# Output product of an RWKV-7 + SoLU kernel: products 320 columns wide in one run, and another order of a slot's transposes

## The chip, the cores and the metric

One core of one Trainium2 chip. The metric is the device time of one execution in microseconds (us). Three runs of the kernel before are on record: 533.9, 535.26 and 539.12 us, median 535.26 us. One further execution was taken with the hardware profiler; its span from the first to the last instruction is 536.5 us, which is 1.2 us above the median and within the spread of the runs.

## The reference

All arrays are float32 at first; the two weight matrices of the second part arrive as 64-bit floats and are converted in the kernel. The first part is a recurrence over 768 time steps for 4 batches and 8 heads of width 40; its output is laid out as 3072 rows of 320 columns and goes through a second part with 1024 hidden columns.

```
for t in range(S):                                   # S = 768
    y[:, :, t] = einsum('bhd,bhde->bhe', r_t, state)
    Sa = einsum('bhde,bhe->bhd', state, a_t)
    state = state * w_t - einsum('bhd,bhe->bhde', Sa, b_t) + einsum('bhd,bhe->bhde', v_t, k_t)
x = y.transpose(0, 2, 1, 3).reshape(3072, 320)
h = x @ w_in                                         # 320 x 1024
solu = h * softmax(h)
ln = (solu - mean(solu)) / sqrt(var(solu) + 1e-6) * g_ln
out = ln @ w_out                                     # 1024 x 320
```

## The kernel before

**Tiling.** The recurrence is cut into chunks of 64 steps. Two batches are worked at once, one on partitions 0 to 63 and one on 64 to 127, so there are N = 24 chunks (12 in time, 2 pairs of batches), each with 8 heads. Each chunk gives 128 rows of the second part. The order of all work on every engine is the order in which the program is written; nothing is rescheduled.

**Slots.** The main loop (L973) runs over slots i = -1 to 26. In one slot several chunks are in different stages: chunk i+5 has its a and b turned (`front`, `front_b`), chunk i+6 its decay (`decay_turned`), chunk i+7 its running sum of log decays (`decay_by_halves`); chunk i+1 has its k, v, r and the state turned (`attend_kv`, `attend_r`, `stated`), its scores and its solution prepared; chunk i is solved and read (`solved`, `read`, `summed`); chunk i-2 goes through `x @ w_in` (`hidden`) and the softmax and variance (`highest`, `exped`, `weighed`, `spreadof`); chunk i-3 has its normalised rows turned (`folded`, tile `lnT`) and multiplied by the output weights (`output`, tile `po`). The inverse that each chunk needs is worked out in small steps on VectorE (L508, L516, L519) which `vector(plan)` puts between the rest.

**Names.** PE (TensorE) turns a tile by `nc.tensor.transpose` into PSUM, and ScalarE (ACT) or VectorE (DVE) copies it to SBUF. The `turned` helper (L395 to L403) issues eight transposes for one operand. In the trace the destination names are: `pa` for a and b, `pkv` for k and v, `plnT` for the normalised rows, `pst` for the state and for the running sum (`pst<-lw`), `pb` for r and for the decay (`pb<-cst,ei`). The copies out of PSUM are `aT` and `bT` on DVE and `kvT`, `rT`, `ex`, `lnT`, `s`, and then `ei` and `inv` (both from the running sum) on ACT. `osb` is the scaled output product on its way from `po` to the output DMA. Then come `pu` (`solved`), `ps` (`scores`), `h` (`hidden`), `psr`, `py`, `px` and `pyo`.

**PSUM.** It is used as four pairs of banks by tag: A, B, C and h. From slot 5 on, B and C change places every slot under the names X and Y. In a slot, `pkv`, `pu` and `py` and the output product `po` at its end use Y; `pb`, `ps` and `px` use X; `pa`, `pst`, `psr` and `pyo` use A; `plnT` and `h` use the tag h, and so does the scrap output of the square `sq` (L790). A tile of a tag can be written when all readers of the tile before it in that tag have ended. `po`, written into Y at the end of one slot, is in the pair that is X in the next slot: `pb` of that slot comes after `osb` has read it.

**The output product.** `output` (L845) adds eight products over f, each of 128 rows of the hidden width by 320 output columns. `in_parts` (L289) splits each into two of 160 columns. A float32 product stands in the trace as two matmul records and two weight loads, so the eight products are 32 records (`po<-w,lnT ... 128x160`, 768 in all). With `FIRST = 6`, slots 5 to 22 issue six of the eight (24 records) at their end, and the other two (8 records) in the next slot, after the transposes of a, b, k and v; the closure `stored` then issues `osb` and the output DMA.

**The end of the loop.** Slot 25 issues seven of the eight products and slot 26 the rest; slot 26 also has the output product of the last chunk in its own function.

The lines of the loop that set the order, from slot 5 on, are L1012 to L1040.

Of the kernel before, what the change touches and what calls it, by code (L numbers as in the profile page):

```python
# [21 lines left out]
AHEAD = 5  # L22
LANDS_NEXT = {2: 6, 3: 7, 4: 8, 5: 11, 6: 9, 7: 10, 8: 12}
LAG = 2
EARLY = 10
NK = 5
FIRST = 6
SPLITS = {2: (0, 0, 0, 2, 4), 24: (0, 0, 0, 0, 2)}


# [23 lines left out]
def kernel(  # L54
# [24 lines left out]
    N = NPAIR * NCH  # L79
    NF = DFF // P  # L80
# [60 lines left out]
    w2 = const.tile([P, NF, DM], FP32, name="w2")  # L141
# [3 lines left out]
    def pair(tag, name):  # L145
        return psum.tile([P, 2, 512], FP32, tag=tag, name=name)
# [142 lines left out]
    def in_parts(o, lhsT, rhs, start, stop, n=2):  # L289
        width = rhs.shape[-1] // n  # L290
        for x in range(n):
            part = slice(width * x, width * x + width)
            mm(o[:, part], lhsT, rhs[:, part], start and not x, stop)
# [119 lines left out]
    def decay_turned(i, t=None, y=0):  # L413

        if not ok(i):
            return lambda: None
        ex = st[i]["ex"] = ex_t[i % (AHEAD + 2)]
        t = turned(pair("B", "pei") if t is None else t, y, ei_t[0])
        return lambda: nc.scalar.copy(out=ex[0:W2, :, :, 1:], in_=t)
# [165 lines left out]
    def attend_r(i, t, y):  # L585
        if not ok(i):
            return lambda: None
        t = turned(t, y, r_t[0])

        def evict():  # L590
            st[i]["rT"] = kept("rT", t)
        return evict
# [252 lines left out]
    def output(i, t, first=NF):  # L845
        if not ok(i):
            return
        d = st[i]
        bp, ci = where_(i)
        t = t[:, 0:DM]  # L850

        def products(lo, hi):
            for f in range(lo, hi):
                in_parts(t, d["lnT"][:, f, :], w2[:, f, :], f == 0, f == NF - 1)
        products(0, first)

        def stored():
            osb = two.tile([P, DM], FP32, tag="osb", name="osb", bufs=1)
            nc.scalar.mul(out=osb, in_=t, mul=d["rs"])
            for p in range(2):  # L860
                nc.sync.dma_start(out=out.rearrange("(b s) n -> b s n", b=B)[2 * bp + p, ci * C:ci * C + C], in_=osb[half(p)])
        if first < NF:
            rest.append((lambda: products(first, NF), stored))
        else:
            stored()
# [107 lines left out]
    for i in range(-1, N + LAG + 1):  # L973
        j, c = i + AHEAD, i - LAG
        plan = plans.get(i, plans[N + i % GRP])
        if len(plan) > 6:
            plan, unflipped = plan[:2] + plan[3:], plan[2]
        else:
            unflipped = ""
        steady = i >= EARLY - AHEAD  # L980
        if i >= 0 and not steady:
            load_keys(j + 3, "w")
        if not steady:
            load_r(i + 3)
        elif i > EARLY - AHEAD and i % GRP:
            load_r(i + 2)
        if i == -1:
            load_values(2)
            land(4, nc.sync)
            land(len(lands), nc.sync)  # L990

        if i < EARLY - AHEAD:
            tc_, ta = pair("C", "pa"), pair("A", "pb")
            front_out, r_out = front(j, ta, 0), attend_r(i + 1, ta, 1)
            fold_out = folded(c - 1)
            ei_out, b_out = decay_turned(j + 1, tc_, 0), front_b(j, tc_, 1)
            kv_out = attend_kv(i + 1, pair(turn["X"], "pkv"))
            r_out()
            front_out()
            if i < EARLY - AHEAD:  # L1000
                vector(plan[0])
                fold_out()
                b_out()
            else:
                b_out()
                vector(plan[0])
                fold_out()
            s_out = stated(i + 1, pair("A", "pst"), 0) if ok(i + 1) else lambda: None
            for evict in (ei_out, kv_out, s_out):
                evict()  # L1010
        else:
            turn.update(zip("XY", ("BC", "CB")[(i - EARLY + AHEAD) % 2]))  # L1012
            ta = pair("A", "pa")
            front_out, b_out = front(j, ta, 0), front_b(j, ta, 1)
            kv_out = attend_kv(i + 1, pair(turn["Y"], "pkv"))
            front_out()
            kv_out()
            b_out()
            if i == N + LAG:
                fold_out = folded(c - 1)  # L1020
            for products, stored in rest:
                products()
                if i == N + LAG:
                    late.append(stored)
                else:
                    stored()
            rest.clear()
            vector(plan[0])
            if i < N + LAG:
                fold_out = folded(c - 1)  # L1030
            ts = pair("A", "pst")
            s_out = stated(i + 1, ts, 0) if ok(i + 1) else lambda: None
            tc_ = pair(turn["X"], "pb")
            r_out, ei_out = attend_r(i + 1, tc_, 0), decay_turned(j + 1, tc_, 1)
            if i == EARLY - AHEAD and ok(j + 2):
                logged(j + 2)
            cum_out = decay_by_halves(j + 2, ts)
            for evict in (r_out, ei_out, fold_out, s_out, *late):
                evict()
            late.clear()  # L1040
        if not steady:
            left(i - 1)
        if i == EARLY - AHEAD:
            load_keys(j + 3, "w")

        early = i < EARLY - AHEAD or i > N - 2
        waves = (1, 0, 1, 0, 1, 0, 1, 1, 0, 0, 0) if early else (0, 0, 2, 1, 0, 0, 1, 1, 0, 0, 0)
        wave = iter(range(NK))

        def run(x):  # L1050
            for _ in range(waves[x]):
                hidden(c, next(wave))
            if sum(waves[:x + 1]) == NK and sum(waves[:x]) < NK:
                highest(c)

        run(0)
        if i >= EARLY - AHEAD:
            cum_out()
        solved(i)()
        vector(plan[1])  # L1060
        if not steady:
            load_keys(j + 2, "bak")
        run(1)
        scores(i + 1)()
        vector(unflipped)
        flip(i + 1)
        run(2)
        scaled(j + 1, "b")
        stated_r(i + 1)
        run(3)  # L1070
        norm(j)
        if ok(j) and j % GRP == GRP - 1:
            begin_inverse(j // GRP)
        scaled(j + 1, "k")
        by_value(i + 2)
        run(4)
        if i == LAG + 1:
            mean = mean_more(pair("A", "pmean")[:, 0], 6, NF, mean)
        carried(i + 1)
        run(5)  # L1080
        read(i, 0)
        if i >= 0:
            load_values(i + 3)
        if steady:
            left(i - 1)
            load_keys(j + 2, "ba" if i % GRP else "b")
            if i % GRP:
                load_r(i + 3)
        ahead = 2 + (i >= EARLY - AHEAD)
        if ok(j + ahead):  # L1090
            logged(j + ahead)
        vector(plan[2])
        run(6)
        couple(i + 1)()
        if i == LAG + 1:
            centred(mean)
        run(7)
        close(i + 1)
        run(8)
        driven(i + 1)()  # L1100
        run(9)
        read(i, 1)
        run(10)
        exped(c)
        vector(plan[3])
        finish = summed(i)
        vector(plan[4])

        if i < EARLY - AHEAD:
            decay(j + 2, pair("C", "pcum")[:, 0])()  # L1110
        tb = pair(turn["X" if i < EARLY - AHEAD else "Y"], "po")
        weighed(c)
        if i == N - 1:
            finish()
        spreadof(c)
        if i >= 0:
            some(Q, (i + 2) // GRP)
            odd = steady and i % GRP == 1
            if odd:
                load_keys(j + 2, "k")  # L1120
                load_keys(j + 4, "w")
            bring(i + 2)
            if odd:
                load_keys(j + 3, "ak")
                load_keys(j + 5, "w")
        if i != N - 1:
            finish()
        vector(plan[5])
        if i == N + LAG:
            output_last(c - 1)  # L1130
        else:
            output(c - 1, tb[:, 0], NF - 1 if i == N + LAG - 1 else FIRST if EARLY - AHEAD <= i < N - 1 else NF)
        if i == -1:
            turn_g(tb[:, 0])
        if i == LAG - 1:
            mean = mean_more(tb[:, 0], 0, 3)
        if i == LAG:
            mean = mean_more(tb[:, 0], 3, 6, mean)
# [30 lines left out]
```

## Time and profile before

| | |
|---|---|
| runs | 533.9, 535.26, 539.12 us; median 535.26 us |
| span of the profiled execution | 536.5 us |
| slots 6 to 17, each from the start of one `po` run to the next | 18.45 to 19.60 us |
| slots 18 to 22, likewise | 17.74, 17.13, 16.95, 16.96 and 16.96 us |
| granted TensorE clock, mean | 0.984 of full speed; 1.00 in every slot from 5 on |
| DVE busy in slots 6 to 17 | 14.97 to 18.86 us of each |
| ACT busy in slots 6 to 17 | 10.93 to 12.00 us of each |

How to read the profile: times are in us from the first instruction. A timeline row has its start, its length, the engine, the line, the operation, output<-inputs with shapes, the count of merged instructions, and in brackets the idle time of the engine just before and what ended it. PE records overlap, since matmuls are pipelined: the start of the next row, not the end of this one, tells how long a row keeps PE. A "busy" PE is therefore not always issuing; a wait shorter than the tail of the last matmul shows no idle time.

### The profile page before, as it was taken

The page shows a single profiled execution, that of the slowest core. Times are in us where ns is not written, and L with a number is a line of the kernel's source. Part 1 is how long each engine was busy: PE and PEld are TensorE (multiplying, and loading weights), DVE is VectorE, ACT ScalarE, POOL GpSimd, SP SyncE. Part 2 cuts the span into 40 slices and gives each one's busy share as a digit, 9 for nine tenths or more (in the row PEclk, how much of TensorE's full clock was granted, in tenths as well). Part 3 has the DMA queues.
Part 4 walks back from the last instruction along what each step waited for, and adds up shares of the span by engine and source line. Part 5 has one row for each costly group of instructions (what it writes and reads, how often), then busy time and mean ns, then how long its engine had stood idle before and what let it go on. Part 6 is the DMA issues. An engine that isn't in the chain of part 4 may idle for free.

```text
span 536.5 us, 28053 instructions
## 1 busy us (share of the span) xinstructions
PE 480.7 (90%) x12029; PEld 391.0 (73%) x12029; DVE 430.6 (80%) x1752; ACT 314.1 (59%) x627; POOL 227.0 (42%) x376
## 2 busy tenths in 40 slices
PE   4633775798989999999999999999999999999997
PEld 3522665665878878877887887788778877887766
DVE  4599987999997987997998979979989888544322
ACT  3633466488457566556666665666656555654433
POOL 4577538245253344545445263544445331210300
PEclk9999978799999999999999999999999999999999
DMA  8898889765465566674774776675554551421210
GB/s 149 153 157 160 177 142 206 165 134 124 90 131 120 102 125 138 123 151 96 147 156 104 132 150 121 118 155 109 114 118 102 108 111 43 106 65 29 61 53 24
DMA packets 194475, 63.95 MB, mean 119 GB/s; under 512 B 166840, under 2 KB 186528, under 8 KB 194352
## 3 DMA queue, kind: packets, MB, share of 16 engines
q1 hardware_dynamic: 181232, 41.60, 41.8%
q0 software_dynamic: 10768, 19.95, 15.2%
q8 instruction: 94, 1.54, 1.2%
q10 hardware_dynamic: 2352, 0.62, 0.7%
q14 instruction: 29, 0.24, 0.2%
HBM read 47.96 MB, written 14.16 MB: 116 GB/s over the span
## 4 chain that ended last, share of the span: by engine, by line
PE 73%; DVE 17%; DMA 5%; issue 2%; ACT 2%; SPq 0%; POOL 0%; ACTq 0%; POOLq 0%; DVEq 0%
PE po L285 20%; PE h L285 18%; PE px L285 6%; PE pyo L285 5%; PE py L285 5%; DVE prod L516 4%; PE ps L285 4%; DVE uu L519 3%; PE pu L285 3%; PE plnT L804 2%; PE pb L400 2%; PE pa L400 2%; PE psr L285 2%; PE pkv L400 2%; DMA uu_dram<-uu 1%
## 5 line engine op out<-in xcount | busy, mean ns | idle before, releaser
L285 PE MATMUL h<-w_in,xT 64*64 64x512 f32 (+1 forms) x1064 | 121.7, 551 | 0.7 <-issue 0.7
L285 PE MATMUL po<-w,lnT 128*128 128x160 f32 x768 | 115.2, 304 | 0.0
L516 DVE TENSOR_TENSOR prod<-blk,uu 128x48 f32<-128x48 f32 (+19 forms) x576 | 108.1, 227 | 1.3
L285 PEld LDWEIGHTS po<-w,lnT 128*128 128x128 f32 x768 | 105.5, 190 | 4.7 <-issue 0.8
L519 DVE TENSOR_TENSOR uu<-uu,prod 128x48 f32<-128x48 f32 (+19 forms) x576 | 103.8, 219 | 0.0
L483 POOL DMA_DIRECT2D nt_dram<-nt x86 | 50.8, 597 | 84.5 <-ACT nt L475 76.4
L792 POOL TENSOR_TENSOR rs<-var,mhalf 128x1 f32<-128x1 f32 x24 | 17.6, 734 | 138.2 <-ACT var L791 138.1
L761 DVE TENSOR_REDUCE nmax<-h 128x1 f32<-128x1024 f32 x24 | 29.3, 1219 | 32.9 <-PE h L285 32.9
L285 PEld LDWEIGHTS h<-w_in,xT 64*64 64x64 f32 x1064 | 36.7, 133 | 20.4 <-issue 16.7
L790 ACT ACTIVATE sq<-e,mu 128x1024 f32<-128x1024 f32 x24 | 26.9, 1119 | 24.4 <-DVE e L777 24.4
L444 DVE TENSOR_TENSOR lu<-pu,cst 128x512 f32<-128x512 f32 x24 | 16.5, 686 | 26.6 <-PE pu L285 24.8
L769 ACT ACTIVATE e<-h,nmax 128x1024 f32<-128x1024 f32 x24 | 26.7, 1111 | 17.7 <-DVE nmax L761 17.7
L558 ACT ACTIVATE wy<-py,cst 128x256 f32<-128x256 f32 x24 | 11.4, 474 | 39.2 <-PE py L285 37.1
L311 POOL DMA_DIRECT2D raw_r<-in_r_dram x48 | 33.3, 698 | 0.0
L777 DVE SCALAR_TENSOR_TENSOR e<-h,e 128x1024 f32<-128x1024 f32 x24 | 29.2, 1217 | 4.3 <-ACT e L769 4.1
L508 DVE SCALAR_TENSOR_TENSOR uu<-blk,uu 128x30 f32<-128x30 f32 (+3 forms) x144 | 30.2, 262 | 1.7 <-DMA blk<-nt_dram 0.8
L393 POOL TENSOR_TENSOR kb<-raw_b,inv 128x320 f32<-128x320 f32 x24 | 21.4, 894 | 21.1 <-DMA raw_b<-in_b_dram 13.7
L285 PE MATMUL pcum<-lw,cst 128*128 128x160 f32 x48 | 15.1, 461 | 16.7 <-ACT lw L351 16.7
L285 PEld LDWEIGHTS py<-tu,nt 64*64 64x64 f32 x768 | 17.3, 142 | 16.3 <-issue 10.7
L617 ACT COPY st<-psr 128x416 f32<-128x416 f32 (+1 forms) x44 | 14.2, 374 | 24.5 <-PE psr L285 24.4
L664 ACT ACTIVATE x<-px 128x832 f32<-128x832 f32 x24 | 20.7, 864 | 11.0 <-PE px L285 11.0
L710 DVE TENSOR_TENSOR tot<-pyo,st 104x416 f32<-104x416 f32 x44 | 23.8, 581 | 2.9 <-PE pyo L285 2.9
(154 smaller groups left out, 1095.3 us busy)
## 6 DMA issues: line engine op xcount, KB each, us to landing
xT<-x_dram SPq DMA_DIRECT2D x48, 160.0 KB, 4.2
blk<-nt_dram POOLq DMA_DIRECT2D x22, 256.0 KB, 4.7
raw_w<-in_w_dram SPq DMA_DIRECT2D x48, 80.0 KB, 3.3
raw_r<-in_r_dram POOLq DMA_DIRECT2D x48, 80.0 KB, 4.0
lv<-in_v_dram SPq DMA_DIRECT2D x48, 80.0 KB, 3.7
out_dram<-osb SPq DMA_DIRECT2D x46, 80.0 KB, 2.5
a<-in_a_dram SPq DMA_DIRECT2D x44, 80.0 KB, 4.0
raw_k<-in_k_dram SPq DMA_DIRECT2D x42, 80.0 KB, 3.8
```

What stands on the lines that cost most here:

```text
L285: nc.tensor.matmul(o, lhsT=lhsT, rhs=rhs, start=start, stop=stop, skip_group_check=True)
L311: queue.dma_start(out=x[half(p), :, 0:D], in_=ap[2 * bp + p, :, ci * C:(ci + 1) * C, :].rearrange("h t d -> t h d"))
L400: nc.tensor.transpose(out=t[0:W2, p, at + C * j:at + C * j + C], in_=x[half(p), 2 * j:2 * j + 2].rearrange("p a b -> p (a b)")[:, skip:ski ...
L483: queue.dma_start(out=blocks[n][e].rearrange("(a x h) s c -> a x s h c", a=GRP, x=2)[at, x], in_=nt[home:home + Q].rearrange("p h j c -> p ...
L508: nc.vector.scalar_tensor_tensor(out=u[:, c, j + 1:Q], in0=nb[:, j, j + 1:Q], scalar=u[:, c, j:j + 1], in1=u[:, c, j + 1:Q], op0=ALU.mult, ...
L516: nc.vector.tensor_tensor(out=ts[-1], in0=nb[:, j:j + 1, j + 1:Q].to_broadcast([P, hi - lo, m]), in1=u[:, lo:hi, j:j + 1].to_broadcast([P, ...
L519: nc.vector.tensor_tensor(out=u[:, lo:hi, j + 1:Q], in0=u[:, lo:hi, j + 1:Q], in1=x, op=ALU.add)
L710: nc.vector.tensor_tensor(out=by_b(tot)[:, :, :, part], in0=y[:, :, :, part], in1=by_b(state_of(i)[:, x])[:, :, :, 0:HW], op=ALU.add)
L761: nc.vector.tensor_reduce(out=nmax, in_=d["h"], axis=AX.X, op=ALU.max, negate=True)
L769: nc.scalar.activation(out=e, in_=d["h"], func=AF.Exp, bias=d["nmax"], accum_out=d["esum"])
L777: nc.vector.scalar_tensor_tensor(out=d["e"], in0=d["h"], scalar=1.0 / DFF, in1=d["e"], op0=ALU.mult, op1=ALU.mult, accum_out=d["mu"])
L790: nc.scalar.activation(out=pair("A" if i == N - 2 else "h", "sq").rearrange("p a b -> p (a b)"), in_=d["e"], func=AF.Square, scale=-float( ...
```

## The change

The diff against the kernel before:

```diff
-FIRST = 6
...
         def products(lo, hi):
             for f in range(lo, hi):
-                in_parts(t, d["lnT"][:, f, :], w2[:, f, :], f == 0, f == NF - 1)
+                mm(t, d["lnT"][:, f, :], w2[:, f, :], f == 0, f == NF - 1)
...
             kv_out()
             b_out()
-            if i == N + LAG:
-                fold_out = folded(c - 1)
+            fold_out = folded(c - 1)
             for products, stored in rest:
                 products()
-                if i == N + LAG:
-                    late.append(stored)
-                else:
-                    stored()
+                late.append(stored)
             rest.clear()
             vector(plan[0])
-            if i < N + LAG:
-                fold_out = folded(c - 1)
+            tc_ = pair(turn["X"], "pb")
+            r_out, ei_out = attend_r(i + 1, tc_, 0), decay_turned(j + 1, tc_, 1)
             ts = pair("A", "pst")
             s_out = stated(i + 1, ts, 0) if ok(i + 1) else lambda: None
-            tc_ = pair(turn["X"], "pb")
-            r_out, ei_out = attend_r(i + 1, tc_, 0), decay_turned(j + 1, tc_, 1)
...
-            for evict in (r_out, ei_out, fold_out, s_out, *late):
+            for evict in (r_out, fold_out, ei_out, s_out, *late):
                 evict()
...
-            output(c - 1, tb[:, 0], NF - 1 if i == N + LAG - 1 else FIRST if EARLY - AHEAD <= i < N - 1 else NF)
+            output(c - 1, tb[:, 0], NF - 1 if i == N + LAG - 1 else NF)
```

- Each of the eight output products of a slot is one product of 320 columns (two records of 128x320) and no longer two of 160.
- In slots 5 to 22 all eight are issued at the end of the slot; none are left for the next slot. (Slot 25 still leaves one.)
- On PE the order at the head of a slot was a, b, k, v, last two products, normalised rows, state, r, decay, running sum. It is now a, b, k, v, normalised rows, r, decay, state, running sum.
- On ACT, `osb` stood behind `kvT` and now stands ahead of it; the order `rT`, `ex`, `lnT`, `s` is now `rT`, `lnT`, `ex`, `s`.
- The orders of DVE, POOL and SP do not change.

## The prediction

> **What bounds the kernel now.** The page came first, for busy shares and the chain of waits.
>
> ```profile
> PE 480.7 (90%) x12029; PEld 391.0 (73%) x12029; DVE 430.6 (80%) x1752; ACT 314.1 (59%) x627; POOL 227.0 (42%) x376
> PE 73%; DVE 17%; DMA 5%; issue 2%; ACT 2%; SPq 0%; POOL 0%; ACTq 0%; POOLq 0%; DVEq 0%
> ```
>
> PE carries the chain that ends last, and from about 163 us on nothing but PE stands in it. Next the table by stretch, one slot each (length, then busy PE, PEld, DVE, ACT, POOL, clock, DMA):
>
> ```profile
> 200.60:219.06 18.46, 18.46 (x509) 15.33 (x509) 14.97 (x56) 11.95 (x25) 11.12 (x17) 1.00 0.63 137
> 219.06:238.66 19.60, 19.17 (x510) 15.68 (x509) 18.86 (x86) 11.87 (x25) 7.61 (x14) 1.00 0.70 133
> ```
>
> Most slots are 18.45 to 18.55 us with PE busy all through: the second is one of two with a stall. So the question is what PE's in-order stream does at the head of a slot. The timeline of slot 7, PE and then ACT:
>
> ```profile
> 200.53 3.53 PE L285 MATMUL po<-w,lnT 128*128 128x160 f32 x24
> 203.99 0.43 PE L400 MATMUL pa<-cst,a 64*104 64x64 f32 x8
> ...
> 204.71 0.39 PE L400 MATMUL pkv<-cst,v 64*104 64x64 f32 x8
> 205.02 1.35 PE L285 MATMUL po<-w,lnT 128*128 128x160 f32 x8
> 206.31 0.71 PE L804 MATMUL plnT<-cst,e 64*128 64x64 f32 x16
> 206.86 0.39 PE L400 MATMUL pst<-cst,st 64*104 64x64 f32 x8
> 207.08 0.40 PE L400 MATMUL pb<-cst,r 64*104 64x64 f32 x8
> 207.31 0.39 PE L400 MATMUL pb<-cst,ei 64*104 64x64 f32 x8
> ...
> 208.87 0.70 PE L285 MATMUL ps<-aT,kvT 40*64 40x64 f32 x32
> ```
>
> ```profile
> 205.13 1.01 ACT L583 COPY kvT<-pkv 104x1024 f32<-104x1024 f32 x1 [0.34 <-PE pkv L400]
> 206.46 0.53 ACT L859 ACTIVATE osb<-po,rs 128x320 f32<-128x320 f32 x1 [0.31 <-PE po L285]
> 207.74 0.58 ACT L410 COPY rT<-pb 104x512 f32<-104x512 f32 x1 [0.75 <-PE pb L400]
> 208.22 0.59 ACT L419 COPY ex<-pb 104x512 f32<-104x512 f32 x1
> 208.70 1.03 ACT L809 COPY lnT<-plnT 128x1024 f32<-128x1024 f32 x1
> ```
>
> The second copy out of `pb`, `ex`, ends at 208.81 and `ps`, which writes the same banks, starts 0.06 later. In every slot from 6 to 17 `ps` starts 0.05 to 0.07 after the end of `ex`. PE shows hardly any idle time there because the tails of `pu` cover it, but ACT sets that start. `rT` itself starts 0.04 after the end of the decay's transposes (207.31 + 0.39 = 207.70), not of r's.
>
> **The products.** The run of 24 takes 3.46 to the next row, that of 8 takes 1.29 (205.02 to 206.31): 2.17 for 16 records, 0.136 each, and 0.20 fixed per run. The only records 320 wide are those of the weight mean:
>
> ```profile
> 121.77 1.78 PE L249 MATMUL po<-w,cst 128*128 128x320 f32 x6
> ```
>
> One of them lasts 0.432, so the spacing is (1.78 - 0.43) / 5 = 0.27 (0.2692 from the starts). Eight products are 16 records: 16 x 0.2692 + 0.20 = 4.51 in one run, where 32 of 160 in one run take 32 x 0.136 + 0.20 = 4.55. Width alone is worth 0.04 a slot; the single run saves a second fixed 0.20 and a change from transposes to full products and back. Head of slot 7: v's transposes to `plnT` is 1.60 now; without the run between it is 0.23, as in slot 5 (168.24 to 168.47). PE's own saving is (3.46 + 1.60) - (4.51 + 0.23) = 0.32 a slot.
>
> [...]
>
> **The transposes and ACT's order.** With v's transposes starting at time v, today's slot 7 has the decay's at v + 2.60 and `ps` at v + 4.16. After the change v moves 1.05 later (4.51 for 3.46). Then: `plnT` +0.23, r +0.55 (its 16), decay +0.23, so the decay starts at v' + 1.01, which is v + 2.06: 0.54 earlier than now. From there ACT decides: tail 0.39 and 0.04 to `rT`, 0.48 to the next copy. That copy is now `lnT`, which holds ACT for 0.90 (208.70 to 209.60), and only then `ex`, 0.59, and 0.06 to `ps`. Sum: v' + 1.01 + 2.46 = v' + 3.47 = v + 4.52. Against v + 4.16 that is 0.36 **later**. PE's own stream would be ready at v' + 2.61 (state 0.23, running sum 0.23 + 0.32, `pu` 0.33, and 0.72 to 0.76 for `pu`, the latter from slots without `ex`); so 0.86 of waiting appears. `kvT` (v' + 0.42, then 0.89) frees ACT by v' + 1.31, ahead of `rT`'s v' + 1.44, so the earlier `osb` costs nothing here. Two new waits on PE are covered: r needs `osb`, done by 5.2 after the `po` start, and r is due at 6.0; `pu` needs `kvT`, seen at v' + 1.5, and is due at v' + 1.9. Behind `ps` on PE wait all of `h`, `psr` and the rest, so the 0.36 is paid in full; from `ps` to the next `po` PE needs 10.12 in undisturbed slots.
>
> **Slot by slot.** Slots 7 and 9 to 17 have this shape: 10 x 0.36 = 3.6. In slot 6 and 8 something is late already. Slot 8: `var` ends at 224.67; then `osb`, `kvT`, `rT`, `lnT`, `ex` run back to back from 224.58 (0.43 + 0.89 + 0.48 + 0.90 + 0.59), `ps` at 227.93 instead of 227.88: +0.05, because waits of 0.24 (`pst` for `bT`) and 0.28 (r for `osb`) go. Slot 6 by the same chain: from `osb` at 187.11, `kvT` at 187.54, and `rT` bound by PE at 188.49, `ps` at 190.52 instead of 190.41: +0.11. Slot 5 has had one run and gains 0.04. Slots 18 to 22 have no decay, so `ps` waits for `rT` alone; there `pu`, which follows `pkv` in its banks, must wait for `kvT` (v' + 1.47), and `ps` comes at v' + 2.2 = v + 3.25 instead of v + 3.47: -0.2 each, -1.0. Five other runs of 32 gain 0.04 each: -0.2. Sum: 3.6 + 0.05 + 0.11 - 0.04 - 1.0 - 0.2 = **+2.5 us**.
>
> **What is pushed.** `aT` and `bT` wait for a and b, 1.05 later. DVE can take it: in every second slot it stands 2.24 idle before `lu`, in the others it works through to the maximum `nmax` and stands 0.67 to 0.96 there (235.62 to 236.29, 272.88 to 273.80); with the slot's own 0.36 that covers 1.05. `plnT` waits for `sq`: it ends by 5.36 after the `po` start (slot 8), `plnT` comes at 5.46. `s` and the copies after it start at once after `ex`, no later than today relative to `ps`. The queues of SP and POOL keep their order; `osb` is ready earlier for its DMA.
>
> **Unseen costs.** PE stood at "issue" inside `py` three times (160.73, 236.78, 348.69), the last making its slot 19.42 instead of 18.46: 0.96. They lie 2031 and 3048 matmul records apart, multiples of about 1016, and the change takes 16 records out of each slot, so they will fall elsewhere. Bounds: none left, about -1.5; four more at 0.96, +3.8; I take 0, as they come by count and not by place. [...]
>
> The sum on the profile's span is 536.5 + 2.5 = 539.0; on the median of 535.26 it is 537.8.
>
> **Rivals.**
> - *Faster: `ps` is not held by `ex`.* Then PE's own readiness counts: v' + 2.61 = v + 3.66, 0.50 earlier than now, in eleven slots -5.5, and with -1.0 and -0.2, 528.6. For it: PE shows no idle time before `ps`. Against: 12 slots with the same 0.06, and the first `h` of the changed order waits for no ACT copy any more, as `ps` already waited past `lnT`.
> - *Faster by the weight loads.* 384 fewer at 0.137 (105.5 / 768), 53 less, 482; against it the spacing of 0.136.
> - *Slower: DVE's delay is not absorbed but comes round as a late softmax.* If `nmax` falls 1.05 later everywhere, `var` ends that much later, and ACT's chain, now without a gap from `osb` to `ex`, passes on what goes beyond 5.44 after the `po` start (`kvT` then starts past v' + 0.42 = 5.65, and the 0.13 by which `rT` waits for PE is used up). Today `var` ends at 5.37, 4.26, 5.68, 4.23, 4.70, 4.39, 4.24, 4.39, 4.96, 4.23, 4.69, 4.47 in slots 6 to 17; plus 1.05 that costs 1.0 + 1.05 (slots 6 and 8) + 0.31 + 0.57 + 0.30 + 0.08 (10, 14, 16, 17) = 3.3 more: 541.1. For it: slot 8 is near that point. Against: the idle stretches above.
>
> **How the numbers follow.** Within 1% is about what measuring this kernel can tell from no change: 529.9 to 540.6. Forecast 0.60, mostly inside (0.52), at times above through further "issue" stops (0.08). DVE rival or a delay of its kind 0.27, above. `ps` not held 0.12 and weight loads 0.01, below. So faster 0.13, same 0.52, slower 0.35. Range: from 531, which leaves out 0.13, to 543.5, the DVE case with 2.4 of further stalls, which leaves out 0.07.
>
> **What would show it.** `po` as x16 in 4.5 with no second run; `lnT` before `ex`; `ps` 0.06 after `ex`, 3.47 after v; slots of some 18.8. A `ps` at v' + 2.6 would refute the main step; `var` later than 5.44 in many slots would show the slower rival; "issue" idle at other tiles the stalls.

## The result and the profile after

The changed kernel takes 539.42 us (median of 7 runs, 537.67 to 540.66), the kernel before 536.28 us on the same chip (7 runs). The ratio is 1.0053 with a 95% interval of 1.0028 to 1.0078: about 3 us slower, inside the range and near the forecast of 537.8.

One thing must be said before the two traces are compared: the profiled execution of the changed kernel has a span of 535.2 us, **shorter** than the 536.5 of before, though its median is longer. A run's time stands 2.06 us or more above its span in every run where both are known, so the span of 536.5 does not lie 1.2 above the median: it fits only the 539.12 us run, the slowest of its seven. The profiled execution of after (537.67 us) is the fastest of its seven. So the spans are cut at the starts of the `po` runs and compared by parts (us; two profiles of each kernel, the second ones from the experiments):

| | up to the `po` that ends slot 4 | slot 5 | slots 6 to 17 | slots 18 to 22 | rest |
|---|---|---|---|---|---|
| before | 163.09 | 18.75 | 224.06 | 85.74 | 44.88 |
| before, again (`e0_before`) | 162.12 | 18.75 | 223.07 | 85.86 | 44.88 |
| after | 160.92 | 18.97 | 225.65 | 84.89 | 44.74 |
| after, again (`e9_changed`) | 162.88 | 18.97 | 230.04 | 84.90 | 44.74 |

The first column differs by up to 2 us between profiles of the same kernel. The stretch that the change reaches, from slot 5 on, is longer in both profiles of after: 374.25 and 378.65 against 373.43 and 372.56.

The page's shares of after, its queue of instructions, and its chain of waits:

```profile
PE 477.0 (89%) x11661; PEld 356.0 (67%) x11661; DVE 434.2 (81%) x1752; ACT 314.6 (59%) x627; POOL 223.2 (42%) x376
...
q8 instruction: 91, 1.49, 1.2%
...
PE 63%; DVE 20%; ACT 10%; DMA 3%; issue 2%; SPq 0%; POOL 0%; ACTq 0%; DVEq 0%; POOLq 0%
```

PE has 368 records fewer (12029 - 11661, 16 in each of 23 runs) and is 3.7 us less busy, but ACT's share of the chain has grown from 2% to 10%. Two slots by stretch (length, then busy PE, PEld, DVE, ACT, POOL, clock, DMA share, GB/s):

```profile
198.73:217.48 18.75, 18.51 (x495) 13.92 (x493) 16.83 (x57) 11.80 (x25) 11.26 (x17) 1.00 0.53 118
217.48:236.23 18.75, 18.50 (x497) 13.91 (x493) 16.76 (x78) 12.02 (x25) 6.42 (x12) 1.00 0.76 141
```

An undisturbed slot was 18.46 and is 18.75: +0.29. The busy time of PE is the same 18.5, and for 0.24 of each slot PE now stands idle, which it did not before. The timeline of PE in slot 7 shows where:

```profile
198.73 4.58 PE L284 MATMUL po<-w,lnT 128*128 128x320 f32 x16
...
203.95 0.39 PE L399 MATMUL pkv<-cst,v 64*104 64x64 f32 x8
204.17 0.66 PE L803 MATMUL plnT<-cst,e 64*128 64x64 f32 x16
204.67 0.39 PE L399 MATMUL pb<-cst,r 64*104 64x64 f32 x8
204.89 0.39 PE L399 MATMUL pb<-cst,ei 64*104 64x64 f32 x8
205.37 0.43 PE L399 MATMUL pst<-cst,st 64*104 64x64 f32 x8
...
207.36 0.69 PE L284 MATMUL ps<-aT,kvT 40*64 40x64 f32 x32 [0.16 <-ACT ex L418]
```

and that of ACT:

```profile
203.39 0.53 ACT L858 ACTIVATE osb<-po,rs 128x320 f32<-128x320 f32 x1 [0.50 <-PE po L284]
204.38 1.02 ACT L582 COPY kvT<-pkv 104x1024 f32<-104x1024 f32 x1 [0.46 <-PE pkv L399]
205.32 0.59 ACT L409 COPY rT<-pb 104x512 f32<-104x512 f32 x1
205.80 1.02 ACT L808 COPY lnT<-plnT 128x1024 f32<-128x1024 f32 x1
206.71 0.60 ACT L418 COPY ex<-pb 104x512 f32<-104x512 f32 x1
```

The eight products are one run of 16 records in 4.51 us (198.73 to 203.24, the start of a's transposes). The decay's transposes start at 204.89, which is 0.94 after v's, so `rT` starts at 205.32; `lnT` then holds ACT from 205.80 to 206.71, `ex` ends at 207.31, and `ps` starts 0.05 later. Idle time before `ps` is charged to `ex` by name, 13 times in slots 5 to 17 (2.8 us; the rest of each wait lies under the tail of `pu`).

### The profile page after: what moved, and what is told of

The parts are those of the page before. It is cut to its first block, busy times and chain, and to the rows that moved or that the text cites. A ratio compares the mean times of both kernels' runs of the same rounds, so it can differ in the third digit from the quotient of the medians.

```text
span 535.2 us, 27321 instructions
## 1 busy us (share of the span) xinstructions
PE 477.0 (89%) x11661; PEld 356.0 (67%) x11661; DVE 434.2 (81%) x1752; ACT 314.6 (59%) x627; POOL 223.2 (42%) x376
## 3 DMA queue, kind: packets, MB, share of 16 engines
q8 instruction: 91, 1.49, 1.2%
## 4 chain that ended last, share of the span: by engine, by line
PE 63%; DVE 20%; ACT 10%; DMA 3%; issue 2%; SPq 0%; POOL 0%; ACTq 0%; DVEq 0%; POOLq 0%
PE po L284 19%; PE h L284 17%; PE px L284 6%; PE pyo L284 5%; PE py L284 5%; DVE prod L515 4%; DVE uu L518 4%; PE ps L284 4%; ACT kvT L582 3%; ACT lnT L808 2%; DVE uu L507 2%; PE psr L284 2%; PE pa L399 2%; ACT rT L409 1%; ACT ex L418 1%
## 5 line engine op out<-in xcount | busy, mean ns | idle before, releaser
L284 PE MATMUL po<-w,lnT 128*128 128x320 f32 (+1 forms) x400 | 109.9, 428 | 0.0
L518 DVE TENSOR_TENSOR uu<-uu,prod 128x48 f32<-128x48 f32 (+19 forms) x576 | 108.6, 228 | 0.0
L515 DVE TENSOR_TENSOR prod<-blk,uu 128x48 f32<-128x48 f32 (+19 forms) x576 | 105.0, 223 | 1.3
L284 PEld LDWEIGHTS po<-w,lnT 128*128 128x128 f32 x400 | 72.3, 190 | 29.3 <-issue 1.2
L791 POOL TENSOR_TENSOR rs<-var,mhalf 128x1 f32<-128x1 f32 x24 | 13.6, 569 | 130.4 <-ACT var L790 130.3
L507 DVE SCALAR_TENSOR_TENSOR uu<-blk,uu 128x30 f32<-128x30 f32 (+3 forms) x144 | 32.3, 277 | 1.8 <-DMA blk<-nt_dram 1.3
L426 DVE TENSOR_TENSOR aT<-pa,ex 104x512 f32<-104x512 f32 x18 | 12.4, 691 | 22.2 <-PE pa L399 19.1
L392 POOL TENSOR_TENSOR kb<-raw_b,inv 128x320 f32<-128x320 f32 x24 | 21.7, 904 | 19.5 <-ACT inv L364 7.0
L284 PE MATMUL ps<-aT,kvT 40*64 40x64 f32 x768 | 17.2, 230 | 13.6 <-ACT kvT L582 10.8
L582 ACT COPY kvT<-pkv 104x1024 f32<-104x1024 f32 x24 | 24.5, 1019 | 5.9 <-PE pkv L399 5.9
```

The source lines that it names most:

```text
L284: nc.tensor.matmul(o, lhsT=lhsT, rhs=rhs, start=start, stop=stop, skip_group_check=True)
L392: nc.gpsimd.tensor_tensor(out=kb[:, j:j + H, 0:D], in0=d["raw_" + n], in1=heads(d["inv"]), op=ALU.mult)
L507: nc.vector.scalar_tensor_tensor(out=u[:, c, j + 1:Q], in0=nb[:, j, j + 1:Q], scalar=u[:, c, j:j + 1], in1=u[:, c, j + 1:Q], op0=ALU.mult, ...
L515: nc.vector.tensor_tensor(out=ts[-1], in0=nb[:, j:j + 1, j + 1:Q].to_broadcast([P, hi - lo, m]), in1=u[:, lo:hi, j:j + 1].to_broadcast([P, ...
L518: nc.vector.tensor_tensor(out=u[:, lo:hi, j + 1:Q], in0=u[:, lo:hi, j + 1:Q], in1=x, op=ALU.add)
L582: return lambda: nc.scalar.copy(out=o[0:W2].rearrange("p b j t -> p b (j t)"), in_=t[0:W2])
```

## The experiments

Each run is timed against the kernel before on the same chip. "Undisturbed" is the slot length that the shortest slots of a kernel share. A "stop" is idle time of PE in a slot, 0.15 us or more, that the profile puts down to "issue", that is, to nothing it shows. The tables and lines are of slots 6 to 17, or of 163 to 410 us.

**The first four.**

`e1_ex_first`: the changed kernel with `ex` ahead of `lnT` again.

```diff
-            for evict in (r_out, fold_out, ei_out, s_out, *late):
+            for evict in (r_out, ei_out, fold_out, s_out, *late):
```

> The changed kernel with the copies back in the order rT, ex, lnT, s; all else as changed. Theory (the scores wait for ex, and ex stands behind the copy of lnT): ex comes 0.9 us earlier, then TensorE's own stream decides (state's transposes after bT, then pu), the scores come 8.1 us after the start of the output run instead of 8.6 (8.3 before the change), some 0.55 us in each of 12 slots, 6.7 us off the changed kernel: about 532.4 us, ratio to before 0.993. Rival (the scores are not held by ex, the loss comes from elsewhere): no difference from the changed kernel, ratio 1.005. Rival (VectorE late): aT and bT stay late, ratio 1.005 or above.

`e2_wide_only`: the kernel before with products 320 wide, nothing else.

```diff
-                in_parts(t, d["lnT"][:, f, :], w2[:, f, :], f == 0, f == NF - 1)
+                mm(t, d["lnT"][:, f, :], w2[:, f, :], f == 0, f == NF - 1)
```

> The kernel before with each output product as one of 320 columns; the split into six and two products and both orders are kept. Theory: two records of 160 take 0.272 us, one of 320 takes 0.269, so 0.04 us a slot, 1 us in all: ratio 0.998, not to be told from 1. Rival (each weight load stands beside no product): 384 fewer loads of 0.137 us, 53 us less, ratio 0.90. Third (stops at issue in TensorE's stream): other instruction counts move them, plus or minus 1.5 us.

`e3_lnT_first_only`: the kernel before with `lnT` ahead of `ex`, nothing else.

```diff
-            for evict in (r_out, ei_out, fold_out, s_out, *late):
+            for evict in (r_out, fold_out, ei_out, s_out, *late):
```

> The kernel before with one edit, the copies in the order rT, lnT, ex, s. Theory: the scores come 0.90 us later in each of the 12 to 13 slots that have a decay, +10.8 us, less what stops and waits of before give back: about 546 us, ratio 1.020; slots 18 to 22 unchanged. Rival (the scores are not held by ex): ratio 1.00.

`e4_one_run_only`: the kernel before with all eight products (160 wide) in one run at the end of the slot; no transpose changes its place, and of the copies only `osb`, which comes ahead of `kvT`.

```diff
-NF - 1 if i == N + LAG - 1 else FIRST if EARLY - AHEAD <= i < N - 1 else NF)
+NF - 1 if i == N + LAG - 1 else NF)
```

> The kernel before with one edit, all sixteen products of 160 columns in one run at the end of slots 5 to 22; transposes and copies keep their order (state, r, decay; rT, ex, lnT), only osb comes ahead of kvT. Theory: a and b, and with them aT and bT, come 1.1 us later; state's transposes then wait for bT to 6.7 us after the start of the run, r and the decay stand behind them, the scores come at 8.7 us instead of 8.3: +0.35 us in 12 slots, -0.15 in 5, about +3.4 us, 539.7, ratio 1.006. Rival (the single run's saving passes through): -0.28 us in 17 slots, -4.8 us, ratio 0.991.

Measured: e1 1.0026 (1.0001 to 1.0050), e2 1.0082 (1.0057 to 1.0108), e3 1.0168 (1.0142 to 1.0194), e4 1.0048 (1.0028 to 1.0067).

e3 bears the theory out. Its ACT timeline, slot 7, and the waits of PE (waiting, releaser, us in total, times, longest):

```profile
208.44 0.59 ACT L410 COPY rT<-pb 104x512 f32<-104x512 f32 x1 [0.75 <-PE pb L400]
208.92 1.02 ACT L809 COPY lnT<-plnT 128x1024 f32<-128x1024 f32 x1
209.82 0.60 ACT L419 COPY ex<-pb 104x512 f32<-104x512 f32 x1
```

```profile
PE ps L285 <- ACT ex L419: 9.3, 13, 1.2
PE pst L400 <- DVE bT L440: 0.5, 1, 0.5
```

One copy moved puts 0.90 between `rT` and `ex`, and an undisturbed slot is 19.37 instead of 18.46: +0.91. The whole of the copy is paid. Nothing else was changed, so `ps` is held by `ex`, and where `lnT` stands on ACT is worth 0.9 us a slot. It also has no stop at all.

e4 also came as expected: undisturbed slot 18.85, because the transposes of the state now wait for `bT`, which is late by as much as a and b have moved:

```profile
PE pst L400 <- DVE bT L440: 3.7, 7, 0.5
PE pst L400 <- DVE prod L516: 3.2, 6, 0.5
PE py L285 <- issue: 0.9, 2, 0.6
```

e1 and e2 missed, by 0.010 each. In e1 `ps` comes at 8.2 us after the `po` start in slot 7 (8.63 in after), and two of its slots are 18.36 long, so the step that it tests is right; but six others are 19.4 to 20.4 long. In e2, which has 0.04 less work per slot, none of the slots 6 to 17 is shorter than 18.55. The waits of PE in e1, then in e2:

```profile
PE pyo L284 <- issue: 3.1, 5, 1.4
PE po L284 <- issue: 0.5, 1, 0.5
PE px L284 <- issue: 0.2, 1, 0.2
PE py L284 <- issue: 0.2, 1, 0.2
```

```profile
PE pyo L285 <- issue: 1.8, 3, 1.4
PE h L285 <- issue: 1.3, 1, 1.3
PE po L285 <- issue: 0.9, 1, 0.9
PE px L285 <- issue: 0.5, 1, 0.5
...
PE py L285 <- issue: 0.2, 1, 0.2
```

These are the "issue" stops that the prediction took as 0, and at tiles that never stopped before. One of e2 in the timeline:

```profile
196.25 0.71 PE L285 MATMUL pyo<-lv,kb 64*64 64x104 f32 x23
198.36 0.48 PE L285 MATMUL pyo<-lv,kb 64*64 64x104 f32 x9 [1.39 <-issue]
```

The run of 32 breaks off after 23 records, though all 32 have the same inputs, so it is hardly data that is missing. Is it the next instruction? The queue that brings PE's instructions (q8 `instruction`) was read from the trace, record by record. It brings 94 packets of 16 KB before and 91 after (1.49 MB). Weight loads and matmuls together are 2 x 11661 = 23322 instructions, 256 to a packet. The packet ahead of this stop started at 196.07 and took 0.95; PE goes on 1.34 after it has landed. Then the instructions (loads, matmuls and the recorded waits of PE's sequencer) were counted up to the one at which PE goes on: 7106, which is 194 modulo 256 (the remainder when it is divided by 256). It is 193 or 194 for each of e1's and e2's stops, and for those of before (9409 and 15553, at `py`).

That gave a new theory: instructions come in blocks of 256, about one block ahead. A block whose work takes less time than it takes to bring the next stops PE at its end. (The place in the program where one block passes into the next is called a block end below.) A slot of before has 508 matmul records, with their loads and 8 counted waits 1024 instructions, four blocks: the block ends stay at the same tiles in every slot (within the transposes, `ps`, `px` and `py`). With 16 records fewer it has 992 (993 in e1 and e2, which have one wait more), and the ends wander through the slot, also into the dense stretch from `py` to `po`.

**The next four** tested it.

`e5_before_63_more`: the kernel before with 63 transposes of 8x8 put in once, early, at a place where PE is idle; nothing reads them. The products and all orders are those of before; only the count is shifted by 126.

```diff
-        t = (h_pair("pcum") if t is None else t)[:, 0:DM]
+        t = h_pair("pcum") if t is None else t
+        for _ in range(63 if i == 5 else 0):
+            nc.tensor.transpose(out=t[0:8, 512:520], in_=ident[0:8, 0:8], identity=ident[0:8, 0:8])
+        t = t[:, 0:DM]
```

> The kernel before with 63 tiny transposes (8x8, nothing reads them) where TensorE stands idle for 5.3 us at 35 to 40 us. No work of the slots changes. Theory (TensorE's instructions arrive in blocks of 256, one block ahead, and a block whose work takes less than some 3.7 us makes it stop): a slot is 1024 instructions, so its four blocks keep their place; before they take 4.6, 4.15, 3.7 and 6.0 us. Moved by 63 matmul records they take 3.65, 3.84, 3.0 and 8.0: a stop of some 0.7 us in each of 12 slots, at the same count modulo 256, 6 to 10 us more, ratio 1.011 to 1.019. Rival (the stops are chance, or belong to a tile): the small transposes are hidden, ratio 1.000.

`e6_ex_first_halves`: e1 with products 160 wide, so one run, the new transposes, `ex` first, and 1025 instructions per slot (`mm(` becomes `in_parts(` again).

> The changed kernel with the copies rT, ex, lnT, s and with each product in two of 160 columns again, still in one run. 1024 instructions a slot, so its blocks keep their place: 3.55, 4.15, 3.7 and 6.8 us. Theory (e1 lost its gain to stops because 992 instructions a slot let the blocks wander into short stretches): 0.27 us less than before in 12 slots and 0.15 in 5, 4 us, less 1 to 3 us of stops at the 3.55 block: ratio 0.993 to 0.998. Rival (e1 lost it to something else in its order): ratio as e1 or above, 1.003.

`e7_ex_first_halves_17`: e6 with the added lines of e5, 17 transposes instead of 63, to shift the count by 34.

> e6 with 17 tiny transposes at 35 to 40 us, which move the blocks by 17 records to 3.8, 4.1, 3.8 and 6.6 us. Theory: hardly a stop is left, 4 us less than before, ratio 0.992 to 0.995, and below e6. Rival (place of the blocks does not matter): as e6.

`e0_before`: the kernel before, profiled again.

> The kernel before, unchanged, for a second profile. Theory: its stops at issue in slots 6 to 17 stand at the same place of the slot (py), at counts equal modulo 1024; how many of the twelve show one varies with how long each fetch takes. Rival (chance): stops at other tiles.

Measured: e5 1.0085 (1.0058 to 1.0111), e6 0.9962 (0.9943 to 0.9982), e7 0.9977 (0.9959 to 0.9995), e0 one run of 536.78 beside a median of 536.64.

e5 is less slow than expected, but slower beyond doubt, although in the slots that were timed nothing but the count is different. Its stops from slot 4 on stand at counts 5569, 13761, 15809 and 18882, again 193 or 194 modulo 256, and now at another tile:

```profile
311.80 0.52 PE L285 MATMUL pyo<-lu,kb 64*64 64x104 f32 x11
313.07 0.58 PE L285 MATMUL pyo<-lu,kb 64*64 64x104 f32 x13 [0.75 <-issue]
```

So where the block ends fall costs time by itself. From slot 4 on e0 has one stop, at `py` at 159.77, near the first of the three of before (160.73).

e6 is faster than both kernels. Its undisturbed slot is 18.40, only 0.06 below before: `ex` no longer decides there, but the wait of `pst` for `bT` seen in e4 stays (decay to state 0.47 instead of the 0.22 that the transposes take), and PE goes from `pu` to `ps` without a gap. e7's profile shows what the shift was meant for, one short wait and no stop in slots 6 to 17 (221.76 for them, against 223.96 in e6's profile), but it missed its expected 0.992 to 0.995, and its median is not lower than e6's. The two intervals overlap, and e7's profile is the second fastest of its ten runs and e6's the second slowest of its ten, so the two profiles do not tell what the shift is worth.

**The next three** take the change apart.

`e8_changed_halves`: the changed kernel with products 160 wide, 1024 instructions per slot (`mm(` becomes `in_parts(`).

> The changed kernel with each product in two of 160 columns again (1024 instructions a slot); the single run, the order of transposes and the copies rT, lnT, ex, s stay. Theory: the wait for ex before the scores, 0.3 to 0.5 us in each slot, also gives the instruction blocks time to arrive, so the changed kernel paid hardly a stop for its width; undoing the width changes little: slots of 18.8 us, ratio to before 1.004 to 1.007. Against e10, which differs in the order of ex and lnT alone: 0.4 us in 12 slots, 0.009 of the ratio. Rival (the change lost its time to the width, as e2 did): ratio 0.997 or below.

`e9_changed`: the changed kernel again.

> The changed kernel once more, on the same chip as e8 and e10: ratio 1.003 to 1.008 as before.

`e10_best`: e6 again.

> e6 once more, on the same chip as e8 and e9: ratio 0.994 to 0.998 as before, if it is faster than both kernels.

Measured: e8 1.0047 (1.0027 to 1.0066), e9 1.0083 (1.0065 to 1.0101, just above what was expected), e10 0.9962 (0.9948 to 0.9977). e8 and e10 differ in the order of `ex` and `lnT` alone: 0.0085, or 4.6 us in the run, with undisturbed slots of 18.79 and 18.40. ACT and then PE of e10 in slot 7:

```profile
206.59 0.58 ACT L409 COPY rT<-pb 104x512 f32<-104x512 f32 x1
207.07 0.59 ACT L418 COPY ex<-pb 104x512 f32<-104x512 f32 x1
207.54 1.03 ACT L808 COPY lnT<-plnT 128x1024 f32<-128x1024 f32 x1
```

```profile
206.16 0.39 PE L399 MATMUL pb<-cst,ei 64*104 64x64 f32 x8
206.63 0.43 PE L399 MATMUL pst<-cst,st 64*104 64x64 f32 x8
...
208.18 0.23 PE L284 MATMUL ps<-aT,kvT 40*64 40x64 f32 x2
```

`ex` ends at 207.66 there, and `ps` starts at 208.18, behind most of `pu`, without waiting for ACT.

e9 and e8 differ in the width: the narrow products cost 0.04 more per undisturbed slot (18.79 against 18.75, as predicted), and yet e8 is the faster by 0.0036, with intervals that just touch. e9's profile shows stops that fit; its waits of PE:

```profile
PE ps L284 <- ACT ex L418: 2.6, 12, 0.7
PE pyo L284 <- issue: 1.5, 3, 0.6
PE po L284 <- issue: 0.4, 2, 0.2
```

The first profile of the same kernel showed no stop in those slots (225.65), this one shows them (230.04, which is 5.0 above 12 x 18.75): its five stops stand at counts 7106, 9410, 15042, 15298 and 17346. So the block ends say where PE can stop, not that it will.

When the block ends are counted in the same way through slots 6 to 17 of all fourteen profiles, 664 of them, PE never enters a block sooner than 1.20 us after the packet with its instructions has landed, and at the 35 stops it enters within 1.20 to 1.56. So a stop comes where the packet starts late or takes long for the block that PE is in:

| block that ends in `pyo` | its successor's packet starts, us into the block | packet takes | PE goes on, us after the landing | block lasts |
|---|---|---|---|---|
| after, slot 14 | 0.27 | 0.88 | 1.83 | 2.98 |
| e9, slot 14, stop of 0.53 | 1.52 | 0.96 | 1.28 | 3.76 |
| e5, slot 15 | 0.17 | 1.29 | 1.43 | 2.89 |
| e5, slot 17, stop of 0.80 | 1.68 | 0.99 | 1.45 | 4.11 |

The block of e9 is 0.78 longer and its stop is 0.53: the rest, 0.25, is the tail of the last matmul (a `pyo` record lasts 0.25 in after). The 3.7 us expected of e5 are not a limit: blocks of 2.98 and 2.89 pass without a stop. In e5 the `pyo` block ends of all twelve slots stand 1.21 to 1.49 after the landing, so PE goes on close to the shortest time seen, 1.20, there in every slot, though only three show a stop.

**The last one** puts the count back without touching the width.

`e11_ex_first_padded`: e1 with 16 transposes of 8x8 in each slot from 5 on, and 16 once ahead of them, as in e5. One more wait is recorded in each slot than before, as in e1, so it has 1025 instructions.

```diff
             tc_ = pair(turn["X"], "pb")
+            for _ in range(16):
+                nc.tensor.transpose(out=tc_[0:8, 0, 256:264], in_=ident[0:8, 0:8], identity=ident[0:8, 0:8])
             r_out, ei_out = attend_r(i + 1, tc_, 0), decay_turned(j + 1, tc_, 1)
```

> The first run of `ex` ahead of `lnT` (products 320 wide, 992 PE instructions per slot, five stops at `pyo`) with 16 transposes of 8x8 in every slot from 5 on, between the normalised rows and r, and 16 more once in the decay of chunk 5 ahead of slot 5: 1024 instructions per slot again, with the products still 320 wide. Nothing reads what the added transposes write. One costs 0.027 us (63 in 1.72), 0.44 per slot, of which up to 0.23 to 0.48 lies in the wait of `pst` for `bT`. Theory of the blocks: the `issue` stops at `pyo`, `h` and `po` in slots 6 to 17 go (at most two short ones at `py` or `px` stay), no slot is over 19.5, the slots are alike at 18.4 to 18.8, slots 6 to 17 together take 222.5 to 227 instead of 229.0, and the ratio is 0.996 to 1.004. Rival, that the wide products bring the stops by what they do themselves (their shape, their loads): the stops stay, some 5 to 7 us of them in slots 6 to 17, and with 0 to 0.2 per slot more the stretch takes 229 to 232, the ratio is 1.003 to 1.009.

Measured: 1.0191 (1.0153 to 1.0230), far above both expectations. Most of that is the price of the padding itself in places that the expectation left out: in slots 18 to 22 it lies on the path (87.45 against 85.18 in e1), and in the last slots it must wait for `osb` to leave the banks (rest 48.97 against 44.75); the part up to slot 4 was also 2.3 longer. So the time decides nothing. In slots 6 to 17, which the two theories are about, the profile reads (waits, 163 to 420 us):

```profile
PE py L284 <- issue: 1.6, 3, 0.7
PE ps L284 <- issue: 0.4, 1, 0.4
```

All stops at `pyo` and `po` are gone, with products as wide as in e1. Four are left instead of e1's seven, at counts 7874, 9410, 13506 and 15554: at `ps` and `py`, the tiles at which before, e4, e6, e8 and e10 stop. At most two were expected, and no slot over 19.5; two are 19.52 and 19.90. The loss beyond undisturbed slots falls from 8.7 (229.01 - 12 x 18.36) to 4.3 (228.51 - 12 x 18.68), not to nothing. Each of the two profiles is of its kernel's slowest run.

The kernels together (lost: slots 6 to 17 less 12 undisturbed ones). A profile is one execution, so the column scatters; the last column tells how far the profiled run lies above the median of its kernel's runs. Where `ex` comes first, slot 17 is shorter by itself (17.87 in e7 and e10), so e1, e6 and e10 have lost some 0.5 more than the column says. Instructions are counted with the recorded waits: one wait more or less moves the block ends by 12 instructions in 12 slots.

| kernel | instructions per slot | undisturbed slot | slots 6 to 17 | lost | stops at | profiled run above the median |
|---|---|---|---|---|---|---|
| before / e0 | 1024 | 18.46 | 224.06 / 223.07 | 2.5 / 1.6 | `py` / none | 2.8 / single run |
| e3 | 1023 | 19.37 | 233.68 | 1.2 | none | 0.5 |
| e4 | 1025 | 18.85 | 228.67 | 2.5 | `py` | 0.8 |
| e6 / e10 | 1025 | 18.40 | 223.96 / 222.59 | 3.2 / 1.8 | `py`, `ps` / `py` | 1.6 / -0.3 |
| e8 | 1024 | 18.79 | 227.10 | 1.6 | `py` | -1.3 |
| e11 | 1025 | 18.68 | 228.51 | 4.3 | `py`, `ps` | 1.4 |
| e5 | 1024, shifted | 18.46 | 226.25 | 4.7 | `pyo` | 0.5 |
| after / e9 | 992 | 18.75 | 225.65 / 230.04 | 0.6 / 5.0 | none / `pyo`, `po` | -1.8 / 0.7 |
| e1 | 993 | 18.36 | 229.01 | 8.7 | `pyo`, `po`, `py` | 3.3 |
| e2 | 993 | not seen | 229.16 | | `pyo`, `po`, `px`, `py` | 1.6 |

## Why the prediction was right, and where it was off

- **`ps` set by ACT, `lnT` ahead of `ex`: right.** v' to `ps` is 3.41 (203.95 to 207.36) where 3.47 was worked out, and `ps` starts 0.05 after `ex`. The slot pays 0.29 instead of 0.36; the missing 0.07 is mostly r, which follows the normalised rows' transposes after 0.50 (204.17 to 204.67) instead of 0.55. e3 shows the term by itself (0.91 for 0.90) and e8 against e10 shows it in the changed kernel.
- **PE's own stream "ready at v' + 2.61": too early.** The transposes of the state write the banks that `bT` is read from. `bT` ends 6.49 after the `po` start in the undisturbed slots of after, and `pst` starts at 6.64, 0.48 behind the decay where 0.23 was worked out; the prediction counts two new waits on PE and leaves this third one out. With `ex` out of the way (e10) `ps` comes at v' + 2.96, so ACT costs 0.45 a slot and not 0.86. For the forecast this made no difference, as ACT was later still; for the rival it did: not 0.50 a slot was to be gained, but the 0.06 to 0.10 that e10 and e1 show.
- **Rival "`ps` is not held by `ex`": refuted** by e3 and by the rows of after. **Rival weight loads: refuted.** 16 records of 320 columns take 4.51, as worked out from a spacing of 0.2692, with loads of 0.190 each between them. This spacing is twice the 0.136 of half the width, and 16 loads fewer make an undisturbed slot 0.04 shorter (18.79 in e8, 18.75 in after), where the rival's 0.137 each would make it 2.2.
- **Rival DVE: refuted.** `var` ends 5.35, 4.16, 4.42, 4.46, 4.82, 4.45, 4.24, 4.36, 4.42, 4.46, 4.44 and 4.46 after the `po` start in slots 6 to 17 of after, all below the 5.44 from which it would count, and at most 0.23 later than in the same slot of before, though `bT` ends 1.05 later (6.49 for 5.44): DVE took most of the delay up. The mechanism itself exists: in e6, `var` ends at 6.14 and 6.00 in slots 6 and 16, and `ps` is 0.38 and 0.24 late in them.
- **Slots 18 to 22: right.** -1.0 was predicted; they take 84.89 and 84.90 against 85.74 and 85.86, so -0.8 to -1.0. In the undisturbed ones PE waits for `kvT` at `pu`, as worked out, and they are 16.77 instead of 16.96 long:

```profile
429.64 0.94 PE L284 MATMUL pu<-x,tu 64*64 64x104 f32 x32 [0.16 <-ACT kvT L582]
```

- **Slots 6 and 8: worked out from one execution.** The delay of slot 8 is not in the second profile of before: `ps` comes 8.34 after the `po` start in e0, where it came at 8.89. Slot 6 has its delay in both, and after is 0.05 later there (8.63 for 8.58), where 0.11 was worked out.
- **Slot 5: wrong in sign, and small.** -0.04 was predicted; it is 0.22 longer (18.97 for 18.75). Its run was single before, but the copies and transposes at its head change like all others, which the step left out.
- **"Unseen costs ... I take 0, as they come by count and not by place": this step was mis-sized.** By count is right. But the count is taken modulo blocks of 256, and whether a block end hurts depends on the place and on when the packet starts: before has its ends at the same four places of every slot, the changed kernel lets them wander. In the first profile of after this cost nothing (0.6 lost against 2.5), in the second 5.0 were lost; e9 against e8 puts the mean at 0.0036 of the time or 1.9 us (the width saves 0.04 a slot besides, so the stops cost some 2.5 more than e8's), within the bounds of -1.5 to +3.8 that were given. The 1016 matmul records, of which the distances between the stops of before are about multiples, are two slots of 508: a stop comes back at the same tile because the slot is four whole blocks.
- **Width "worth 0.04 a slot": right for the work (18.79 to 18.75), wrong for the time**: e2, width alone, is 0.0082 slower, and the same edit takes 32 instructions out of a slot. That the count and not the width itself brings the stops is what e5 and e11 speak for.
- **The sum.** Undisturbed slots 12 x 0.29 = 3.5, slot 5 +0.2, slots 18 to 22 -0.8 to -1.0, rest -0.1: +2.6 to +2.8 by parts, where +2.5 was predicted. The medians differ by 3.1. The difference of 1.6 between 537.8 and 539.42 is thus mostly the base: the median of before was 536.28 over seven runs and not 535.26. The agreement of the sum is in part luck: slots 6 to 17 were put 0.3 too high and slot 5 0.26 too low, and the stops, put at 0, left 0.3 to 0.5 in this comparison, but 1.4 to 1.6 in that of e9, where the medians differ by 4.2.

That after came out at 1.0083 when it was timed again (e9) and at 1.0053 at first (intervals overlapping) is left open; how often the stops fall may differ from chip to chip, which these runs can't tell.

**A version that beats both** is e6 (run again as e10): one run of eight products, 160 wide, the new order of the transposes, and the copies as `rT`, `ex`, `lnT`, `s`. It measured 0.9962 twice (0.9943 to 0.9982 and 0.9948 to 0.9977), 2.3 and 2.5 us below before. The gain in the change was real, and the order of two copies took it away.

## What to carry to other kernels

When a transpose is moved earlier on PE, look at the copy that empties its banks: the order of the copies on ACT decided here when the banks could be written again, and one long copy ahead of a needed short one was paid in full (e3: `lnT`, which holds ACT for 0.90, made the undisturbed slot 0.91 longer). Taking instructions out of a loop that PE fills without gaps is not free of risk: if the loop's count was a whole number of instruction blocks (here 1024, four packets of 256), the block ends start to move, and can come to lie in a dense stretch (992 here: 0.6 us lost in slots 6 to 17 of one profile of after and 5.0 in the other); compare the "issue" stops of several executions, not of one, and see where the profiled run stands among the timed ones. A profile whose span contradicts the medians is cut into parts and compared stretch by stretch.

## What the runs showed of the hardware

- PE's instructions come in packets of 16 KB, 256 instructions each (2 x 11661 in 91 packets after, 2 x 12029 in 94 before). From slot 4 on, the "issue" stops at `py`, `pyo`, `px`, `po`, `psr`, `h` (e2) and inside `ps` all end at a count of 193 or 194 modulo 256 (before, e0, e1, e2, e4, e5, e6, e8, e9, e10, e11), 1.2 to 1.6 us after a packet has landed; a packet takes 0.9 to 1.8 us. Why it is 193 or 194 was not shown. The "issue" idle times ahead of `pb` at 79 to 107 us, before the slots in question, stand at other counts.
- The next packet is not sent far ahead: in slots 6 to 17 it mostly starts 0.1 to 2.2 us after PE has entered the block before it. At none of the 664 block ends there does PE go on sooner than 1.20 us after the landing. So whether the same block end stops PE depends on when the packet starts and how long it takes in that execution; what makes it start was not found out.
- Most block ends cost nothing here: in slots 6 to 17 PE stopped at 35 of the 664, for up to 1.4 us (e1, e2). Shifting them alone (e5) makes the kernel 0.0085 slower.
